# FFN2 products beside the last pair's seven-product gate and val: whole array in place of quarters

## The chip, the cores and the metric

The kernel runs on one core of one Trainium2 chip. The metric is the device time of that core in microseconds; the profile is one execution of the program, recorded on the chip. The engines are TensorE (PE for matmuls, PEld for its weight loads), VectorE (DVE), ScalarE (ACT), GpSimd (POOL) and SyncE (SP).

## The reference

Attention with a sigmoid in place of the softmax, then a SwiGLU block; batch 8, 12 heads, 448 tokens, head size 64, d_model 768, d_ff 1536, all in fp32 at the borders.

```python
scores = scale * np.matmul(q, k.transpose(0, 1, 3, 2)) - np.log(S)
attn = 1.0 / (1.0 + np.exp(-scores))
attn_out = np.matmul(attn, v)
x = attn_out.transpose(0, 2, 1, 3).reshape(B * S, H * D)      # 3584 x 768
g = x @ w_gate                                                # 3584 x 1536
silu = g * (1.0 / (1.0 + np.exp(-g)))
out = (silu * (x @ w_val)) @ w_out                            # 3584 x 768
```

## The kernel before

The work is cut by batch element (448 tokens) and, for the second matrix product, by pair of batch elements (896 tokens, four pairs m = 0 to 3).

**Attention.** For each batch element and each group of four heads, `burst` computes scores in quarters of the array (64 x 64 blocks, four matmuls at a time), `sig` applies the sigmoid on ScalarE, and `pv` multiplies with v. The results become the transposed x tiles `xT`.

**Gate and val (FFN1).** For batch elements 0 to 5, `f1` computes gate and val for two column blocks f and f + 1 together in quarters. For the last pair (elements 6 and 7), `f1_pair` uses a scheme of seven block products in place of eight: sums and differences of x tiles (`xsum`, on VectorE) and of weight blocks (`f1_sums`, made earlier, parked in DRAM and loaded back into the staging buffers by `wload`) are multiplied, and the products are added up again. `one_set(f)` issues, for each f of six, seven products of gate and seven of val. Each product is three matmuls of 128 x 128 weights by 448 columns on the whole array (line 727). Between them, products are copied out of PSUM by ScalarE (`snap`, line 741), added by VectorE (`add`, line 756), passed through the SiLU by ScalarE (`silu`, line 766) and multiplied by VectorE (`fin`, lines 775 and 778), which gives `hT`.

**FFN2.** For pair m, `f2_set(m, k)` handles two token tiles of 128 (`e`, the even, and `o`, the odd), again with seven products for eight. Each product contracts six blocks of 128 with 384 output columns. Products 5 and 6 use sums of hT tiles, s1 and s2, made by VectorE (lines 886 and 889); product 7 needs s3 (line 892), product 3 needs s4 (line 959). The results are taken out of PSUM by ScalarE (product 1, line 952) and VectorE (the others, line 912, the operations u2, u3, u4, c11, c12, c21, c22), and stored by DMA (line 922) from GpSimd's queue, or from SyncE's and ScalarE's for the last pair.

A product can be issued in two ways. `f2_single` issues six matmuls of 128 x 128 weights by 384 columns (line 903). `f2_pair` issues two products together in quarters, by `quarters` (line 549): 48 matmuls of 64 x 64 weights by 384 columns in two halves of 24. In each half two rows of quarters work on different products, and the second half exchanges the rows. The first matmuls of the second half wait for a `turn` (line 531), an empty instruction on ScalarE that waits for the last matmuls of the first half. Both products are evacuated after the second half.

**Order of work.** All work is first recorded as `op` objects with an engine, an estimated duration, dependencies and buffers. `list_schedule` then plays the list through with these estimates and writes out each engine's instructions in the order that comes of it. PSUM banks (tag "P", eight of them) are given to whoever is first able to start. The planner adds SWITCH = 0.094 us when TensorE changes between the whole array (mode "F") and quarters (mode "Q"), and while in quarters it prefers to remain there. FFN2 items stand in the list `f2q`; in the last stretch up to MIX = 3 items are recorded behind each f of the last pair's gate and val, and KEEP = 3 are held back for the end. This happens in the block that starts when `i == NQ and sl == 3`. The items issued there are those of pair m = 2; pair m = 3 comes last, and was issued by `f2_single` already.

Of the kernel before, what the change touches and what calls it, by code (L numbers as in the profile page):

```python
# [66 lines left out]
MARGIN = 1.0  # L67
# [131 lines left out]
def kernel(  # L199
# [17 lines left out]
    NS = 7  # L217
    QB = H // 4
# [8 lines left out]
    one = ctx.enter_context(tc.tile_pool(name="one", bufs=1))  # L227
# [44 lines left out]
    def op(*a, **kw):  # L272
        o = Op(*a, **kw)
        ops.append(o)
        return o
# [23 lines left out]
    R = {}  # L299
# [98 lines left out]
    def tr_pe(i, n, parts=None, split=False):  # L398

        ins = R[("cq", "ck")[n], i]  # L400
        parts = parts or [("DVE", 0, NS)]

        def fpe(s0, s1):
            def fn():
                if s0 == 0 or split:
                    T["tr", i, n] = bank("ps_tr").bitcast(BF16)[:, 0:NS * 128].rearrange("p (s c) -> p s c", s=NS)
                T["tr", i, n, s0] = T["tr", i, n]
                for s in range(s0, s1):
                    nc.tensor.transpose(out=T["tr", i, n][:, s, :],
                                        in_=src16[i % NSRC][:, n, s].rearrange("p a d -> p (a d)"),  # L410
                                        identity=idn)
            return fn

        def fm(eng, s0, s1):
            def fn():
                if n == 0 and s0 == 0:
                    qkT_tile(i)
                cp(eng, T["qkT", i][:, n, s0:s1], T["tr", i, n, s0][:, s0:s1])
            return fn
        for k, (eng, s0, s1) in enumerate(parts):  # L420
            a = op("PE", 0.06 * (s1 - s0), fpe(s0, s1),
                   deps=[(ins[min(k, len(ins) - 1)], -MARGIN if i > QB else 0.0)],
                   take=["P"] if s0 == 0 or split else [], give=R["cq", i][0].take if n and s1 == NS else [])
            if s0 == 0 or split:
                taken = a.take
            m = op(eng, 0.1 + (0.53 if eng == "DVE" else 0.8) * (s1 - s0) / NS, fm(eng, s0, s1), deps=[a],
                   take=["qkT"] if n == 0 and s0 == 0 else [], give=taken if s1 == NS or split else [])
            R.setdefault(("qkT", i), []).append(m)
            R["qkT", i, n, s0] = m
# [193 lines left out]
    NC = KC // 2  # L623
# [35 lines left out]
    def f1_pair(m):  # L659

        b0, b1 = 2 * m, 2 * m + 1
# [15 lines left out]
        def xsum(k, j):  # L677
            e0, e1, o0, o1 = (lambda: T["xT", b0, j]), (lambda: T["xT", b0, NC + j]), \
                (lambda: T["xT", b1, j]), (lambda: T["xT", b1, NC + j])
            out, x, y, f = {1: (lambda: tile_of(1, j), o0, o1, ADD),  # L680
                            2: (lambda: tile_of(2, j), lambda: tile_of(1, j), e0, SUB),
                            3: (o0, e0, o0, SUB),
                            4: (lambda: tile_of(4, j), e1, lambda: tile_of(2, j), SUB)}[k]
            deps = [R["xT", b, q] for b in (b0, b1) for q in (j, NC + j)] + quiet
            X[k, j] = op("DVE", 0.36, lambda: nc.vector.tensor_tensor(out=out(), in0=x(), in1=y(), op=f),
                         deps=deps + [X.get((k - 1, j))], take=["xT"] if (k, j) == (4, 2) else [])

# [168 lines left out]
    def f2_set(m, k):  # L856
# [51 lines left out]
        def add(name, n, dst, other, deps, free=True, first=None):  # L908
            def fn():
                if first:  # L910
                    first()
                nc.vector.scalar_tensor_tensor(out=c(*dst), in0=T["p", m, k, n], scalar=HREC, in1=c(*other), op0=MULT, op1=ADD)  # L912
            C[name] = op("DVE", 0.45, fn,
                deps=[P[n]] + deps, give=taken[n] if free else [])
# [26 lines left out]
        def after(n, final):  # L941

            def result(t):
                T[("osb",) + t] = staging("osf")[:, 0:DM] if final else \
                    sb.tile([128, DM], FP32, tag="osb", bufs=slots["osb"], name=f"osb_{t[0]}_{t[1]}")

            if n == 1:
                def fn(cols):
                    def go():
                        if cols == lo:  # L950
                            result(e)
                        nc.scalar.activation(out=c(e, cols), in_=T["p", m, k, 1], func=COPY, scale=HREC)
                    return go
                C["p1"] = op("ACT", 0.45, fn(lo), deps=[P[1]], take=["osf" if final else "osb"])
                C["p1b"] = op("ACT", 0.45, fn(hi), deps=[C["p1"]], give=taken[1])
            elif n == 6:
                add("u2", 6, (e, hi), (e, hi), [C["p1b"]])
            elif n == 2:
                C["s4"] = op("DVE", 0.56, lambda: nc.vector.tensor_tensor(
                    out=blk(e, 1), in0=blk(e, 1), in1=T["s", 2, m, k], op=SUB), deps=[P[2], C["s2"]])  # L960
                add("c11", 2, (e, lo), (e, lo), [C["p1"]])
                if end:
                    store(e, [C["c11"]], [], final, lo)
            elif n == 7:
                add("u3", 7, (o, lo), (e, hi), [C["u2"]], first=lambda: result(o))
                C["u3"].take = [Slot("osf" if final else "osb")]
            elif n == 5:
                add("u4", 5, (e, hi), (e, hi), [C["u3"]], free=False)
                add("c22", 5, (o, hi), (o, lo), [C["u3"]])
                P[5].give = P[5].give + C["s1"].take  # L970
                if end:
                    store(o, [C["c22"]], [], final, hi)
            elif n == 3:
                add("c12", 3, (e, hi), (e, hi), [C["u4"]])
                store(e, [C["c11"], C["c12"]], C["p1"].take, final, hi if end else slice(0, DM))
            elif n == 4:
                add("c21", 4, (o, lo), (o, lo), [C["u3"], C["c22"]])
                store(o, [C["c21"], C["c22"]], C["u3"].take, final, lo if end else slice(0, DM))
            R.setdefault(("f2", m), []).append(P[n])
        return dict(start=start, product=product, after=after, spec=spec, P=P, taken=taken, key=(m, k))  # L980

    def f2_pair(x, y):

        two = (x, y)
        key = x[0]["key"] + x[1:]

        def make(final):
            for f, n in two:
                if n == 1:
                    f["start"](final)  # L990

            def fn(t):
                def go():
                    if t == 0:
                        for q, (f, n) in enumerate(two):
                            T[("p",) + f["key"] + (n,)] = bank("ps_o", q)[:, 0:HW]
                    quarters([[(T[("p",) + f["key"] + (n,)], f["spec"][n][0]()[:, x // 2, x % 2], f["spec"][n][1](x))
                              for f, n in two] for x in range(NH)], HALVES, t, key)
                return go
            a = None  # L1000
            for t in range(2):
                a = op("PE", 0.1625 * NH, fn(t), mode=("Q", "Q"), take=[] if t else ["P", "P"],
                       deps=[d for f, n in two for d in f["spec"][n][2]()] + ([turn(a, key + (0,))] if t else [(x, LAT["PE"] + LATE) for x in [R.get("turn")] if x]))
                banks = banks if t else a.take
            R["turn"] = a
            for q, (f, n) in enumerate(two):
                f["P"][n] = a
                f["taken"][n] = banks[q:q + 1]
            for f, n in two:
                f["after"](n, final)  # L1010
        return make

    def f2_single(f, n):

        def make(final):
            if n == 1:
                f["start"](final)
            f["product"](n, final)
            f["after"](n, final)
        return make  # L1020
# [78 lines left out]
    for i in range(NQ + QB + 2):  # L1099
        att = i < NQ  # L1100
        for sl in range(4):
# [50 lines left out]
            while len(f2q) > (KEEP if fpos == NPLAIN * NF else 0) and f2acc >= f2q[0][0] and ("ws", 4, NH - 2) in R:  # L1152
                w, fn = f2q.pop(0)
                f2acc -= w
                fn(False)
            if i == NQ and sl == 3:
                sums, wload, one_set = f1_pair(B // 2 - 1)
                sums()
                todo = [(nm, f) for f in range(NH) for nm in "gv"]
                for x in todo[:5]:  # L1160
                    wload(*x)
                last = None
                for f in range(NH):
                    last = one_set(f, last)
                    for _ in range(min(MIX, len(f2q) - KEEP)):
                        f2q.pop(0)[1](False)
                    for x in todo[5 + 2 * f:7 + 2 * f]:
                        wload(*x)
# [46 lines left out]
```

## Time and profile before

| what | value |
|---|---|
| median of 3 runs | 403.71 us (402.93 to 409.8) |
| profiled execution, its own time | 403.9 us |
| span of the profiled execution | 402.1 us |
| granted TensorE clock, mean | 1.000 |
| TensorE busy | 394.9 us (98%) |
| VectorE / ScalarE / GpSimd busy | 254.2 / 243.6 / 136.2 us |
| DMA | 76.91 MB, mean 191 GB/s |
| last pair's gate and val begin | 299.8 us after the span's start |
| FFN2 of the last pair, first line 903 product | 369.35 us |

The busy time of an engine is the time in which at least one of its instructions ran. Matmuls overlap: one of 64 x 384 shows 0.33 us though the next step starts 0.16 us later, so rates are read from start to start. A view called the chain of work follows what ended last back from the last instruction, to whatever released each step. L549, L727 and so on are lines of the kernel.

### The profile page before, as it was taken

How to read it: one execution, taken by the hardware profiler on the slowest of the kernel's cores; microseconds unless marked ns; L12 is line 12 of the kernel's file. 1: busy time of each engine (PE TensorE's matmuls, PEld its weight loads, DVE VectorE, ACT ScalarE, POOL GpSimd, SP SyncE). 2: the span in 40 equal slices, each digit the busy share in tenths (PEclk: the TensorE clock that was granted, in tenths of full speed). 3: DMA queues.
4: the chain of work that ended last, by engine and by line, in shares of the span. 5: the costliest groups of instructions: out<-in, count | busy, mean ns of one | idle time of the engine just before them, and what ended most of it. 6: DMA issues, size and time to landing. Idle time of an engine off the chain costs nothing.

```text
span 402.1 us, 15922 instructions
## 1 busy us (share of the span) xinstructions
PE 394.9 (98%) x6973; PEld 270.7 (67%) x6973; DVE 254.2 (63%) x492; ACT 243.6 (61%) x509; POOL 136.2 (34%) x202
## 2 busy tenths in 40 slices
PE   8999999999999999999999999999999999999995
PEld 3546657667797787799777866666885555555663
DVE  3525544546786465755866857576668666658874
ACT  5996687757766852766668666767726434663110
POOL 1788865565455223424234332402020202000100
PEclk9999999999999999999999999999999999999999
DMA  8999999999776629759678688853004325100535
GB/s 277 379 375 377 374 301 268 315 304 284 221 203 186 160 52 276 170 178 261 163 211 224 202 223 223 191 215 102 22 14 123 104 82 156 42 0 2 159 88 147
DMA packets 67989, 76.91 MB, mean 191 GB/s; under 512 B 35920, under 2 KB 61264, under 8 KB 67920
## 3 DMA queue, kind: packets, MB, share of 16 engines
q1 hardware_dynamic: 63952, 62.93, 54.4%
q0 software_dynamic: 1920, 7.87, 7.7%
q10 hardware_dynamic: 2048, 5.11, 3.3%
q8 instruction: 54, 0.88, 0.9%
q14 instruction: 15, 0.12, 0.1%
HBM read 51.90 MB, written 15.73 MB: 168 GB/s over the span
## 4 chain that ended last, share of the span: by engine, by line
PE 85%; DMA 11%; POOL 1%; SPq 1%; issue 0%; DVE 0%; POOLq 0%; ACTq 0%
PE ps_v L549 19%; PE ps_g L549 18%; PE ps_o L549 17%; PE ps_o L903 7%; PE ps_sc L452 6%; PE ps_pv L495 6%; DMA st<-in_v_dram 6%; PE ps_g L727 6%; PE ps_v L727 6%; DMA st<-in_moe_w_gate_dram 5%; SPq L325 1%; POOL v L295 1%; POOL wg L366 1%; DVE st L912 0%; POOLq L295 0%
## 5 line engine op out<-in xcount | busy, mean ns | idle before, releaser
L473 ACT ACTIVATE pt<-ps_sc 128x448 f16<-128x448 f32 x336 | 163.0, 552 | 57.6 <-PE ps_sc L452 57.1
L549 PE MATMUL ps_v<-xT,wv 64*64 64x448 f16 x1728 | 103.0, 349 | 0.4 <-issue 0.3
L549 PE MATMUL ps_g<-xT,wg 64*64 64x448 f16 x1728 | 101.7, 349 | 0.3 <-POOL wg L366 0.2
L549 PEld LDWEIGHTS <-wg 64*64 64x64 f16 x1728 | 66.2, 107 | 21.6 <-issue 1.1
L452 PE MATMUL ps_sc<-qkT 64*64 64x448 bf16 x672 | 80.4, 351 | 0.1
L549 PEld LDWEIGHTS <-wv 64*64 64x64 f16 x1728 | 65.7, 107 | 21.1 <-issue 1.9
L579 DVE TENSOR_TENSOR t<-ps_g,s 128x448 f16<-128x448 f32 x72 | 43.1, 620 | 52.1 <-ACT s L573 51.4
L549 PE MATMUL ps_o<-wo,hT 64*64 64x384 f16 x888 | 72.4, 324 | 0.1
L295 POOL CAST src<-st 128x896 bf16<-128x896 f32 (+1 forms) x43 | 41.4, 966 | 70.5 <-DMA st<-in_q_dram 33.1
L549 PEld LDWEIGHTS <-hT 64*64 64x64 f16 x1080 | 50.5, 107 | 11.7 <-issue 3.5
L295 POOL CAST v<-st 64x448 f16<-64x448 f32 (+1 forms) x72 | 41.0, 569 | 48.2 <-PE ps_pv L495 35.0
L586 DVE SCALAR_TENSOR_TENSOR hT<-ps_v,t 128x448 f16<-128x448 f32 x72 | 41.7, 618 | 23.4 <-PE ps_v L549 22.0
L922 POOL DMA_DIRECT2D out_dram<-osb x40 | 20.8, 525 | 96.4 <-DVE osb L912 96.2
L573 ACT ACTIVATE s<-ps_g 128x448 f16<-128x448 f32 x72 | 37.0, 549 | 23.1 <-PE ps_g L549 13.0
L495 PE MATMUL ps_pv<-pt,v 64*64 64x448 f16 x672 | 46.9, 350 | 0.1
L549 PE MATMUL ps_o<-st,s 64*64 64x384 f16 x480 | 46.3, 323 | 0.0
L912 DVE SCALAR_TENSOR_TENSOR osb<-ps_o,osb 128x384 f32<-128x384 f32 x70 | 36.6, 551 | 10.8 <-PE ps_o L549 9.0
L452 PEld LDWEIGHTS <-qkT 64*64 64x64 bf16 x672 | 35.1, 106 | 11.1 <-issue 2.4
L495 PEld LDWEIGHTS <-v 64*64 64x64 f16 x672 | 26.8, 107 | 9.9 <-issue 2.3
L549 PEld LDWEIGHTS <-s 64*64 64x64 f16 x480 | 29.1, 107 | 5.1 <-issue 1.5
L293 DVE CAST xT<-ps_pv 128x448 f16<-128x448 f32 x40 | 23.4, 618 | 12.6 <-PE ps_pv L495 11.0
L727 PEld LDWEIGHTS <-st 128*128 128x128 f16 x144 | 13.8, 98 | 13.6 <-issue 1.2
(78 smaller groups left out, 391.0 us busy)
## 6 DMA issues: line engine op xcount, KB each, us to landing
st<-in_q_dram SPq DMA_DIRECT2D x24, 448.0 KB, 5.5
st<-in_v_dram SPq DMA_DIRECT2D x24, 448.0 KB, 6.8
st<-in_k_dram SPq DMA_DIRECT2D x23, 448.0 KB, 6.1
out_dram<-osb POOLq DMA_DIRECT2D x40, 192.0 KB, 3.5
st<-in_moe_w_gate_dram SPq DMA_DIRECT2D x12, 384.0 KB, 9.0
st<-in_moe_w_val_dram SPq DMA_DIRECT2D x12, 384.0 KB, 8.8
st<-in_moe_w_out_dram SPq DMA_DIRECT2D x12, 384.0 KB, 7.8
tsum<-st ACTq DMA_DIRECT2D x12, 384.0 KB, 4.1
```

The source lines that it names most:

```text
L293: nc.vector.tensor_copy(out=o, in_=i)
L295: nc.gpsimd.tensor_copy(out=o, in_=i)
L452: nc.tensor.matmul(out=sc[a][64 * (g ^ a):64 * (g ^ a) + 64, 0:S].rearrange("k (s p) -> k s p", s=NS), lhsT=kT[r, s, 64 * g:64 * g + 64], ...
L473: nc.scalar.activation(out=T[("pt",) + key][:, a], in_=T[("sc",) + key][a][:, 0:S], func=SIGM, bias=sbias, scale=qkscale)
L495: nc.tensor.matmul(out=T["pv", i, a][64 * g:64 * g + 64, :], lhsT=T["v16", i][r, a, s, :], rhs=T["pt", i, s][r, a, :], start=(s == 0), sto ...
L549: mm = nc.tensor.matmul(out=o[cs], lhsT=w[rs, cs], rhs=x[rs], start=p == 0 and k == 0, stop=p == len(parts) - 1 and k == len(steps) - 1)
L573: nc.scalar.activation(out=t, in_=T["g", b, f], func=SIGM)
L579: nc.vector.tensor_tensor(out=t, in0=T["g", b, f], in1=T["s16", b, f], op=MULT)
L586: nc.vector.scalar_tensor_tensor(out=T["hT", m][:, f, o * S:(o + 1) * S], in0=T["v", b, f], scalar=HSC, in1=T["t1", b, f], op0=MULT, op1=MULT)
L727: nc.tensor.matmul(out=T["fp", key], lhsT=win(nm, f, n)()[:, j], rhs=xin[n](j), start=n in first and j == 0, stop=j == NC - 1, skip_group_ ...
L903: nc.tensor.matmul(out=T["p", m, k, n], lhsT=lhs()[:, x // 2, x % 2], rhs=rhs(x), start=x == 0, stop=x == NH - 1)
L912: nc.vector.scalar_tensor_tensor(out=c(*dst), in0=T["p", m, k, n], scalar=HREC, in1=c(*other), op0=MULT, op1=ADD)
```

## The change

When the last pair's gate and val begin, a flag is set. From then on, an item that would have been a pair in quarters records its two products one after the other through `f2_single`. Three added conditions on the planner's order (a lead of 99 us leaves only "not before it has started") concern transposes, their copies and the operation c22; one on `xsum` would add the last element's `f1` as a dependency, where it has one.

```diff
@@ tr_pe
-                   deps=[(ins[min(k, len(ins) - 1)], -MARGIN if i > QB else 0.0)],
+                   deps=[(ins[min(k, len(ins) - 1)], -MARGIN if i > QB else 0.0)] + [(x, 99.0) for x in R.get(("tr", i, n), [])],
...
+            R.setdefault(("tr", i, n), []).append(a)
...
-            m = op(eng, 0.1 + (0.53 if eng == "DVE" else 0.8) * (s1 - s0) / NS, fm(eng, s0, s1), deps=[a],
+            m = op(eng, 0.1 + (0.53 if eng == "DVE" else 0.8) * (s1 - s0) / NS, fm(eng, s0, s1), deps=[a] + [(x, 99.0) for x in R.get(("qkT", i), [])[:1]],
@@ f1_pair, xsum
-            deps = [R["xT", b, q] for b in (b0, b1) for q in (j, NC + j)] + quiet
+            deps = [R["xT", b, q] for b in (b0, b1) for q in (j, NC + j)] + quiet + R.get(("F1", b1), [])
@@ f2_set, after
-                add("c22", 5, (o, hi), (o, lo), [C["u3"]])
+                add("c22", 5, (o, hi), (o, lo), [C["u3"], (C["u4"], 99.0)])
@@ f2_pair
         def make(final):
+            if R.get("full"):
+                for one in two:
+                    f2_single(*one)(final)
+                return
             for f, n in two:
@@ main loop
             if i == NQ and sl == 3:
+                R["full"] = True
                 sums, wload, one_set = f1_pair(B // 2 - 1)
```

## The prediction

> **What bounds the kernel now.** First I read the busy lines, the clock and the chain that ended last on the page. They say whether any engine but TensorE can matter.
>
> ```profile
> PE 394.9 (98%) x6973; PEld 270.7 (67%) x6973; DVE 254.2 (63%) x492; ACT 243.6 (61%) x509; POOL 136.2 (34%) x202
> ...
> PEclk9999999999999999999999999999999999999999
> ...
> PE 85%; DMA 11%; POOL 1%; SPq 1%; issue 0%; DVE 0%; POOLq 0%; ACTq 0%
> ```
>
> TensorE is busy in 98% of the span at the full clock. The DMA part of the chain lies at the start (transfers up to 49.4 us). So a microsecond of TensorE time saved later is a microsecond of the end, unless it becomes a wait. Next I read the chain in order of time where the changed products run, from 306.8 us on (start, length, what):
>
> ```profile
> 305.70 0.57 PE ps_g L727 x3
> 306.26 0.57 PE ps_v L727 x3
> 306.83 1.10 PE ps_o L549 x24
> 307.93 0.67 PE ps_g L727 x3
> 308.61 0.57 PE ps_v L727 x3
> 309.17 0.57 PE ps_g L727 x3
> 309.74 0.57 PE ps_v L727 x3
> 310.31 2.07 PE ps_o L549 x48
> 312.38 0.68 PE ps_g L727 x3
> 313.06 2.07 PE ps_o L549 x48
> 315.13 0.68 PE ps_v L727 x3
> ...
> 365.99 2.10 PE ps_o L549 x48
> 368.09 0.02 issue
> 368.11 0.02 ACTq L531
> 368.14 0.04 issue
> 368.18 1.17 PE ps_o L549 x24
> 369.35 28.39 PE ps_o L903 x174
> ```
>
> The chain stays on TensorE from 299.8 to 397.75 us. A group "L549 x24" is one half of a pair (24 quarter products), "L727 x3" one product of the last pair's gate or val, "L903 x6" one FFN2 product on the whole array. Three prices stand here. A whole-array FFN2 product costs 28.39 / 29 = 0.979 us. A gate or val product after another costs 0.567 us. The first one after quarters costs 0.67 to 0.68. A lone half costs 1.10.
>
> **The change, part by part.** The instruction order of the built changed kernel shows where it acts. Up to the half at 306.83 us every engine's instructions and waits are the same; GpSimd's and SyncE's are the same to the end. So the new scheduling conditions on transposes, sums and c22 move nothing: zero, by that order. From 306.83 us on, nine pairs (18 halves, 432 quarter matmuls) become 18 whole-array products (108 matmuls). The 74 gate and val products left there stay. Where halves stood in groups of 1, 2, 2, 1, the products now stand in groups of 1 and 5.
>
> *Bare products: nothing gained.* A half does the arithmetic of one product. In the timeline of the last halves its four quarters advance by 0.16 us per step (368.37, 368.53, 368.69), six steps, 0.96 us; the whole-array product takes 0.976 from start to start (370.27 to 371.24). The array was as full before as it is after.
>
> *Going in and out of quarters: the gain.* Before, TensorE left the whole array for quarters 12 times from 306.83 on: seven lone halves, four groups of two, and a last group of three.
> - Lone half: 1.10 - 0.979 = 0.12 going in, and 0.675 - 0.567 = 0.11 on the product after it: 0.23, seven times, 1.61 us.
> - Group of two: 2.07 - 1.958 = 0.11, and 0.11 behind it: 0.22, four times, 0.89 us.
> - Last group: 368.18 + 1.17 - 365.99 = 3.36 us for three halves, less 2.94 = 0.42 us. It holds the one wait on ScalarE's turn mark (368.09 to 368.18), as the last half had nothing between it and the one whose end it needs.
>
> Sum: 1.61 + 0.89 + 0.42 = 2.9 us. The other way: the stretch 306.83 to 369.35 is 62.5 us; filled with 74 x 0.567 = 42.0 and 18 x 0.979 = 17.6 it is 59.6. Again 2.9 us.
>
> *What replaces it.* A gate or val product directly beside an FFN2 product on the whole array (24 such borders) does not occur before. Nearest rows: gate to val, which changes bank, weights and operand, adds nothing (0.57 after 0.57), and FFN2 to FFN2 neither (29 products in one stretch). The far end is the border to quarters, 0.11 to 0.12 a side, 2.7 us in all; below zero is excluded, since the products already follow without a gap. I take zero, as the rows without a mode change are nearer, and keep 2.7 for the range.
>
> *Weight loads.* A quarter load took 106 ns and ran beside other quarters; a whole-array load takes 98 ns and must hide behind a 163 ns matmul. In 370 to 397 us there are 168 matmuls in 27.0 us, 0.161 each, with 167 such loads: they hide. The Trainium skill speaks against the change here: "TensorE: Matmul & The Clock Gate", section "Part 3: Packing small matmuls — row/col tiling", says a weight load overlaps running matmuls only when its row group differs, which whole-array products never offer. By that rule alone, 108 loads of 98 ns would stand bare, some 10.6 us, and the kernel would end near 411.6 us. The row of 370 to 397 us contradicts it for this form, so I use the row.
>
> *What hides the evacuation.* VectorE was busy 42.1 of 62.5 us there; in 59.6 us that is 71%. The tight places are the runs of five FFN2 products. In the first, by start distances of before (0.535 us for an accumulate of 448 columns, 0.31 for the f16 multiply, 0.47 for FFN2's), VectorE has three accumulates, one multiply and eight FFN2 operations, 5.7 us, beside 4.9 us of TensorE. It finishes about 1.1 us behind the run's last product. The next gate accumulate needs its own two products and a ScalarE copy, about 0.8 us later still, and each bank that TensorE takes was released more than 0.5 us earlier by the same walk. So: zero. The second run is looser, since its first product (6) has no sums waiting. In the last run (7, 5, 3, 4, then the final pair's 1 and 6) product 6 needs the sum s2. From the end of val's product 7 as zero: s1 6.34 to 6.81, c12 to 7.28, s2 to 7.75; the product would start at 8.12. Before, s2 ended at 369.10, 1.17 us ahead of 370.27. So the cover shrinks to about 0.3 us; if the walk errs, 0.1 to 0.3 us is lost. Then the s3 and s4 that follow are no later relative to TensorE than before.
>
> *ScalarE's queue.* The turn marks of the nine pairs go; one of them is worth 0.09 us, inside the 0.42. Loads and stores keep their order on SyncE and GpSimd and only start up to 2.9 us earlier; DMA share in this stretch is 0.23.
>
> After 369.35 us the order is that of before, so the end moves as a whole: span 402.1 - 2.9 = 399.2. The profiled execution took 403.9, 1.8 more than its span, and the median of the runs is 403.71. By the one the forecast is 401.0, by the other 400.8; I take **400.9 us**, 0.7% faster. About 2% is what a measurement of this kernel can tell from no change (its three runs spread from 402.93 to 409.8), so this is expected to count as the same.
>
> **The rivals.**
> 1. *The borders cost what the quarters' borders cost.* For: no row shows an L727 product touching an L903 one. Against: every border inside the whole-array mode that is shown adds nothing. It gives back 24 x 0.11 = 2.7 us: 403.6 us.
> 2. *VectorE becomes the bound (the slower side).* Place: the three runs of five. If TensorE cannot take a bank until VectorE has caught up, each run costs the 1.1 us that VectorE is behind: 3.3 us, net +0.4, 404.2 us; at twice that lag, 407.6 us. It decides against the change once the three waits sum to over 2.9 us. For: FFN2 products now come five in a row where at most two did, and one VectorE operation evacuates each at 0.47 us besides the sums. Against: eight banks, of which five or six are free as the run begins, and 21.6 busy of 27 us in the last stretch, where 28 products follow each other without a stall.
> 3. *Whole-array weight loads are not hidden.* 108 x 98 ns = 10.6 us, less 2.9: 411.6 us. Against it stands the row of 370 to 397 us.
> 4. *The change does nothing.* Excluded: the built order holds 324 fewer matmuls.
>
> **How the numbers follow.** Forecast, with small losses in the last run: 0.80. Borders: 0.10. VectorE: 0.06. Weight loads: 0.02. Some other gain (a hole closing elsewhere) or loss: 0.02. The range: from 399.9, the forecast less the 1.0 us between the fastest run (402.93) and the profiled one (403.9), to 403.6, the far end of the border cost. Faster by over 2% (under 395.6 us) would need 5 us more than there is: 0.01. Slower by over 2% (over 411.8): 0.02. Within: 0.97.
>
> **What would show it.** Right: no L549 after about 306.8 us; groups of L903 x6 and x30 between L727 groups at 0.98 us a product; every L727 product at 0.57, also behind L903; the final 174 matmuls starting near 366.4 us. Rival 1 would show as 0.67 behind each FFN2 group; rival 2 as waits of TensorE on VectorE in front of ps_o or ps_g groups; rival 3 as L903 products of 1.5 us. I would be wrong if TensorE waited for s2 by over 1 us, or if the granted clock left 1.00 in the longer whole-array stretch; the two such stretches shown (342 to 361 and 370 to 397 us) kept 1.00.

## The result

The changed kernel takes 401.48 us (median of 22 runs, 399.48 to 403.69) against 403.74 us for the kernel before (22 runs, 402.17 to 409.8). The ratio of the two, taken over the fast runs (without the two slowest of before, 408.55 and 409.8 us), is 0.9934, with a 95% interval of 0.9912 to 0.9956: 0.66% faster, some 2.7 us (1.8 to 3.6). That is clear of zero and, by the 2% mark, counts as the same. The profiled execution took 400.04 us, with a span of 398.3 us.

The span is 3.8 us shorter, but not all of that is the change. The first gate product of the last pair, up to which the instructions of the two kernels are the same, starts at 299.84 us before and at 298.84 us here. In the profiles of the runs below it starts between 298.56 and 300.96 us where that part is unchanged. So about a microsecond of the 3.8 belongs to the one execution. I therefore compare a length inside the span: from that first gate product to the start of the last 174 FFN2 matmuls. It was 369.35 - 299.84 = 69.51 us. After, the last 192 matmuls start at 362.67 and run at 31.21 / 192 = 0.1626 us each, so the last 174 start at 365.60 and the length is **66.76 us**: 2.75 us less. A little more lies behind that point: before, the 174 matmuls follow a stay in quarters and take 28.39 us; after, they follow whole-array products and take 28.28 (up to 393.88). From the first gate product to the end of TensorE's work it is 397.75 - 299.84 = 97.91 us before and 393.88 - 298.84 = 95.04 us after: 2.87 us less.

The page of the changed kernel: busy time, share and instructions of each engine, and the granted clock of TensorE.

```profile
PE 391.2 (98%) x6647; PEld 268.2 (67%) x6649; DVE 254.0 (64%) x492; ACT 243.4 (61%) x509; POOL 136.7 (34%) x202
...
PEclk9999999999999999999999999999999999999999
```

TensorE's matmuls are 326 fewer by the records (324 by the built order) and its busy time follows the span; the other engines have the same work. The chain in order of time (start, length, what), through the first stretch that changed and at its end:

```profile
302.42 0.58 PE ps_g L728 x3
...
304.22 1.28 ACT L767
305.50 0.01 issue
305.51 0.58 ACT pt L767
306.10 0.02 issue
306.12 0.39 DVE hT L779
306.51 0.47 DVE s L890
306.98 0.54 DVE pt L757
307.51 0.47 DVE hT L893
307.98 0.55 DVE hT L757
308.52 0.04 issue
308.57 0.73 PE ps_v L728 x3
309.30 4.88 PE ps_o L904 x30
314.17 0.57 PE ps_g L728 x3
...
319.85 0.97 PE ps_o L904 x6
320.82 0.57 PE ps_g L728 x3
...
362.67 31.21 PE ps_o L904 x192
```

(The lines of this kernel named here stand one below those of before: L728 is the gate and val product, L904 the FFN2 product, L757 the accumulate of gate and val.) Five FFN2 products now cost 4.88 us, 0.976 each, and the gate product behind them 0.57, not 0.67 as behind quarters. The detour of the chain through ScalarE and VectorE is new: TensorE waits there. The timeline of TensorE shows how long.

```profile
307.77 0.54 PE L728 MATMUL ps_g<-src,wg 128*128 128x448 f16 x2
308.15 0.35 PE L728 MATMUL ps_g<-xT_s,wg 128*128 128x448 f16 x1
308.57 0.54 PE L728 MATMUL ps_v<-src,wv 128*128 128x448 f16 x2
308.94 0.35 PE L728 MATMUL ps_v<-xT_s,wv 128*128 128x448 f16 x1
309.13 1.14 PE L904 MATMUL ps_o<-wo,hT 128*128 128x384 f16 x6
```

The step after 308.15 is 0.42 us where one matmul takes 0.19: 0.23 us lost in front of val's product 3 of the first f.

### The profile page after: what moved, and what is told of

Read it like the earlier page. It is cut to its first block, busy times and chain, and to the rows that moved or that the text cites. A ratio compares the mean times of both kernels' runs of the same rounds, so it can differ in the third digit from the quotient of the medians.

```text
span 398.3 us, 15268 instructions
## 1 busy us (share of the span) xinstructions
PE 391.2 (98%) x6647; PEld 268.2 (67%) x6649; DVE 254.0 (64%) x492; ACT 243.4 (61%) x509; POOL 136.7 (34%) x202
## 4 chain that ended last, share of the span: by engine, by line
PE 84%; DMA 10%; POOL 2%; DVE 2%; ACT 1%; issue 0%; POOLq 0%; SPq 0%; ACTq 0%
PE ps_v L550 19%; PE ps_g L550 18%; PE ps_o L550 12%; PE ps_o L904 12%; PE ps_pv L496 6%; PE ps_sc L453 6%; PE ps_v L728 5%; PE ps_g L728 5%; DMA st<-in_v_dram 5%; DMA st<-in_moe_w_gate_dram 4%; DMA st<-in_q_dram 1%; POOL wg L366 1%; POOL v L295 1%; ACT pt L474 0%; ACT L767 0%
## 5 line engine op out<-in xcount | busy, mean ns | idle before, releaser
L550 PE MATMUL ps_v<-xT,wv 64*64 64x448 f16 x1728 | 101.8, 350 | 0.0
L550 PEld LDWEIGHTS <-wg 64*64 64x64 f16 x1728 | 65.0, 107 | 22.4 <-POOL wg L366 1.2
L550 PEld LDWEIGHTS <-wv 64*64 64x64 f16 x1728 | 63.9, 107 | 21.7 <-issue 1.0
L453 PE MATMUL ps_sc<-qkT 64*64 64x448 bf16 x672 | 78.1, 351 | 0.1
L550 PE MATMUL ps_o<-wo,hT 64*64 64x384 f16 x648 | 51.9, 323 | 0.1
L550 PEld LDWEIGHTS <-hT 64*64 64x64 f16 x792 | 39.5, 107 | 5.9 <-issue 0.7
L453 PEld LDWEIGHTS <-qkT 64*64 64x64 bf16 x672 | 33.5, 107 | 10.8 <-issue 1.9
L550 PE MATMUL ps_o<-st,s 64*64 64x384 f16 x336 | 32.7, 323 | 0.0
L904 PEld LDWEIGHTS <-hT 128*128 128x128 f16 x186 | 18.1, 98 | 12.5 <-issue 0.4
L904 PE MATMUL ps_o<-wo,hT 128*128 128x384 f16 x138 | 25.7, 326 | 0.0
```

Of the source, the lines that this page charges most:

```text
L453: nc.tensor.matmul(out=sc[a][64 * (g ^ a):64 * (g ^ a) + 64, 0:S].rearrange("k (s p) -> k s p", s=NS), lhsT=kT[r, s, 64 * g:64 * g + 64], ...
L550: mm = nc.tensor.matmul(out=o[cs], lhsT=w[rs, cs], rhs=x[rs], start=p == 0 and k == 0, stop=p == len(parts) - 1 and k == len(steps) - 1)
L904: nc.tensor.matmul(out=T["p", m, k, n], lhsT=lhs()[:, x // 2, x % 2], rhs=rhs(x), start=x == 0, stop=x == NH - 1)
```

## The experiments

All edits are shown against the changed kernel, and each ratio is to the kernel before, run beside it on the same chip, with its 95% interval. Most compare the same length, from the first gate product of the last pair to the start of the last 174 FFN2 matmuls: 69.51 us before, 66.76 after. Where another measure is used, the text says so.

**Pairs kept, but on the whole array (e1).** Each half of a pair is one whole product; the joint banks, the turn mark and the joint evacuation stay.

```diff
-            if R.get("full"):
-                for one in two:
-                    f2_single(*one)(final)
-                return
+            full = R.get("full")
...
+                    if full:
+                        f, n = two[t]
+                        for x in range(NH):
+                            mm = nc.tensor.matmul(out=T[("p",) + f["key"] + (n,)], lhsT=..., rhs=..., ...)
+                            if t and x == 0:
+                                after_ins(mm.ins, T["turn", key + (0,)])
+                        T["end", key + (t,)] = [mm.ins]
+                        return
...
-                a = op("PE", 0.1625 * NH, fn(t), mode=("Q", "Q"), ...
+                a = op("PE", 0.1625 * NH, fn(t), mode=("F", "F") if full else ("Q", "Q"), ...
```

> The nine pairs keep their form (two products recorded together, two banks taken at once, the second product waiting for the turn mark on ScalarE, both evacuated after the second), but each half is one product on the whole array; all work is done. The length compared is from the first gate product of the last pair to the start of the last 174 FFN2 matmuls: 69.5 us before, 66.8 us in the changed kernel. Theory (the gain is the going in and out of quarters): 66.6 to 67.1 us, ratio to before 0.993. Rival (the gain is the end of the joint evacuation and of the turn marks): 69 us or more, ratio 0.999 to 1.002.

Measured: ratio 0.9928 (0.9903 to 0.9952); 367.99 - 300.96 = 67.03 us. The groups stand as before (1, 2, 2, 1), and the chain shows what each of them costs now:

```profile
325.20 1.95 PE ps_o L1002 x12
327.15 0.57 PE ps_g L728 x3
...
364.79 1.96 PE ps_o L1002 x12
366.75 0.02 issue
366.77 0.02 ACTq L532
366.79 0.05 issue
366.84 1.15 PE ps_o L1002 x6
367.99 28.29 PE ps_o L904 x174
```

A group of two takes 1.95 in place of 2.07, and the product of gate or val behind it 0.57 in place of 0.67 to 0.68. So the gain comes with the array's mode, in the old structure too. The only part that the structure keeps is the turn mark of the last group: 0.09 us of waiting and a last half of 1.15 in place of 0.976, together 0.27 us, which is what the length exceeds 66.76 by. (It is one delay: the last half starts at 366.84, 1.24 us behind the product ahead of it, which starts at 365.60. The chain books a part of it to the half, since the recorded ends of matmuls overlap the next starts.)

**Three of nine pairs back in quarters (e5).**

```diff
             if i == NQ and sl == 3:
-                R["full"] = True
...
                     last = one_set(f, last)
+                    R["full"] = f > 0
```

> The flag is set only after the first three pairs beside gate and val, so six of nine pairs are whole-array; all work is done. Theory: four of the twelve stays in quarters come back, two lone halves and two groups of two, 2 x 0.23 + 2 x 0.22 = 0.90 us, less the 0.2 us that TensorE waits in the changed kernel in front of val's product 3 of the first f: 67.3 to 67.6 us from the first gate product to the last 174 matmuls (66.8 in the changed kernel, 69.5 before). Rival (the gain sits in one place, the last group with its turn mark): 66.8 or less.

Measured: ratio 0.9939 (0.9917 to 0.9960). The first gate product starts at 300.52, the last 192 matmuls at 365.05, the last 174, 18 matmuls or 2.93 us later, at 367.98: 67.46 us, inside the 67.3 to 67.6 expected. The gain grows with the number of stays in quarters that are taken away; it doesn't sit in one place.

**Whole array everywhere (e3).** Here the time of whole runs is compared, since products move from one stretch to another.

```diff
+    R["full"] = True
     for i in range(NQ + QB + 2):
```

> The flag is set from the start, so all pairs of FFN2 are issued as single products on the whole array, also those between FFN1's quarters; all work is done. In the built order TensorE changes between quarters and the whole array 74 times in place of 34. Theory: 40 changes at 0.11 us cost 4.4 us against the changed kernel: about 405.4 us, ratio to before 1.004 (1.001 to 1.008), and each such group costs its whole-array time plus about 0.22. Rival (a product on the whole array is cheaper in itself): 25 more pairs gain 0.3 us each, 394 us, ratio 0.975.

Measured: 403.75 us, ratio 1.0007 (0.9991 to 1.0023). The rival is far off: 25 more pairs on the whole array bring no gain but lose most of what nine had gained, some 2.9 us. The chain, where FFN1's and attention's quarters surround the products:

```profile
222.48 0.19 PE ps_sc L453 x4
222.67 2.06 PE ps_o L904 x12
224.72 0.31 PE ps_sc L453 x4
```

Two products take 2.06 (1.95 without a change of mode) and the score matmuls behind them 0.31 in place of 0.19: 0.11 + 0.12 us, the same price from the other side. The size was missed, though: 20 more stays at 0.22 are 4.4 us, and 2.9 (1.8 to 4.0 by the two intervals together) were measured; the ratio lies just under the 1.001 to 1.008 expected. The profiles do not close the gap of 1.5 us. Two val halves of FFN1 that take 1.43 us in place of 1.14 before and after (at 120.71 and 132.74 us after) have no counterpart here, up to 0.6 us; but in the second profile of the changed kernel the first of them takes 1.25, so they differ from one execution to the next. And TensorE stands 0.53 us in front of gate's product 7 of the first f, where it waits on a copy by ScalarE; that is new and makes the gap larger. What fills it is not settled.

**The table of the SiLU loaded early (e4).**

```diff
                 sums()
+                op("ACT", 1.5, lambda: nc.scalar.activation(out=warm, in_=sb_t, func=SILU), deps=R["sigmoids"])
```

> The changed kernel plus one SiLU of a single column on ScalarE, placed after the last sigmoid, so that the table that the first SiLU needs is loaded earlier; all work is done. Theory (the 0.23 us that TensorE stands in front of val's product 3 of the first f comes from that 1.28 us load, through VectorE's queue): the load ends before the first copy of gate's product 1, the wait goes, 66.5 us from the first gate product to the last 174 matmuls against 66.8. Rival (VectorE is late there of itself, by the FFN2 operation that now stands in its queue): the wait stays, 66.7 to 66.8.

Measured: ratio 0.9918 (0.9899 to 0.9938); 363.83 + 2.93 - 300.22 = 66.54 us. The chain has no detour left, and the load stands in a free stretch of ScalarE:

```profile
293.78 1.28 ACT L1165 ACT_TABLE_LOAD   x1
295.08 0.20 ACT L1165 ACTIVATE warm<-sbiast 128x1 f32<-128x1 f32 x1
...
305.48 0.57 ACT L767 ACTIVATE pt<-pt 128x448 f16<-128x448 f32 x1
```

The wait of 0.23 us was the load's: with it gone the length is 2.97 us below that of before, and the stretch to the end of TensorE's work (395.05 - 300.22 = 94.83 us) 3.08 us below. The FFN2 operation in VectorE's queue, the rival, stands behind the accumulate in question and had no part.

**Column halves: another mode than quarters (e6).**

```diff
+                    if cols:
+                        for z in (slice(0, 64), slice(64, 128)):
+                            nc.tensor.matmul(out=T["p", m, k, n][z], lhsT=lhs()[:, x // 2, x % 2][:, z], rhs=rhs(x), ...)
+                        continue
...
+            cols = R.get("cols")
...
             if R.get("full"):
+                R["cols"] = True
                 for one in two:
                     f2_single(*one)(final)
+                R["cols"] = False
                 return
```

> The changed kernel, but each of the 18 products is issued as column halves: two matmuls of 128 x 64 weights by 384 columns, all rows, beside each other; all work is done. The order has eight stays away from the whole array (groups of 1, 5, 1, 5, 1, 1, 1 and 3 products), with no turn marks and no joint evacuation. Theory (leaving and re-entering the whole-array mode costs, whatever the other mode is): 8 x 0.22 = 1.8 us over the changed kernel, 68.3 to 68.8 us from the first gate product to the last 174 matmuls (66.8 in the changed kernel, 69.5 before). Rival (the cost belongs to the quarters with their exchange of rows): 66.8 us. If the two halves don't run beside each other, 18 x 0.98 = 18 us are added instead.

Measured: ratio 0.9973 (0.9954 to 0.9991); 367.00 - 298.76 = 68.24 us, just under the range.

```profile
305.18 0.57 PE ps_v L728 x3
305.74 1.10 PE ps_o L906 x12
306.84 0.67 PE ps_g L728 x3
...
309.21 5.00 PE ps_o L906 x60
314.21 0.67 PE ps_g L728 x3
```

A lone product costs 1.10 and the gate product behind it 0.67, to the digit as with quarters; five cost 5.00 in place of 4.88. The two halves run beside each other. Eight stays at 0.22 are 1.8 us; 1.48 were added. The 0.23 us wait on the table load is gone, as TensorE now comes that much later to val's product 3, and the way back behind the last stay lies in the last 174 matmuls, which take 28.40 us here (395.40 - 367.00) as before. So the price is paid for leaving the whole-array form, whether for quarters or for halves.

The weight loads show where that price sits. Before, the first load for the gate product behind the lone half starts at 307.86 us, together with its matmul (307.86) and after 0.30 us without a load; in the changed kernel the load for the same product starts at 306.48, 0.16 us ahead of its matmul (306.64). It is so at every change of form from the first gate product on, to quarters and back before, to column halves and back here: load and matmul start within 0.01 us of each other, and the step to that matmul is 0.09 us longer than without a change. A load takes 0.10 to 0.11 us. That the price is mainly this one load, no longer hidden, is a reading of these rows; no run here separates it from other causes.

**One more pair, and the early table (e7).** The changed kernel again (e8) ran beside it.

```diff
+            if i == NQ and sl == 2:
+                R["full"] = True
             while len(f2q) > (KEEP if fpos == NPLAIN * NF else 0) and ...
...
                 sums()
+                op("ACT", 1.5, lambda: nc.scalar.activation(out=warm, in_=sb_t, func=SILU), deps=R["sigmoids"])
```

> The changed kernel, the table of the SiLU loaded early as in e4, and the flag set one step earlier, so that the pair of which one half lay alone between the first gate and val products is whole-array too; all work is done. Theory: one more stay goes (0.22 us) and the wait on the table load (0.23 us): 0.45 us less than the changed kernel, ratio to before about 0.992, and no product of gate and val longer than 0.57 us in the profile except the first. Rival (what is saved there comes back as a wait, since seven gate and val products now start in a row): the same as the changed kernel.

> The changed kernel itself, beside e6 and e7 on the same chip: ratio to before 0.991 to 0.996; 66.7 to 66.9 us from the first gate product to the last 174 matmuls, with TensorE's wait of 0.23 us in front of val's product 3 of the first f again (theory), or 66.5 us without it (if that wait was an accident of one execution).

Measured: 0.9949 (0.9932 to 0.9966) for the one with both, 0.9937 (0.9917 to 0.9957) for the changed kernel again. Here the length needs another start, as a product moved ahead of the first gate product: from the last group of attention's 28 matmuls of line 496 it is 364.02 + 2.93 - 294.11 = 72.84 us, and 362.39 + 2.93 - 292.04 = 73.28 us for the changed kernel. The forecast 0.45 us are there in the profile (0.44), and TensorE runs without a wait through the stretch. In the time of whole runs they don't show: the ratio forecast, 0.992, lies outside the interval, and the intervals of e7 and e8 overlap widely, so 0.1% can't be told from them either way. The changed kernel's own length is 365.32 - 298.56 = 66.76 us again, with the same 0.23 us wait (a step of 0.42 at 307.87), so that wait is no accident.

## Why the prediction was right, and what it missed

**Bound and sum.** The forecast was 2.9 us off the end, by the going in and out of quarters; measured are 2.87 us from the first gate product to the end of TensorE's work, and 2.7 (1.8 to 3.6) in the time. The forecast of 400.9 us stands 0.6 below the median. The mechanism is shown by e1, e5 and e6. That 2.87 comes so close to 2.9 is partly luck: with the early table the gain is 3.08, so the sum was some 0.2 us short, and the wait described below took 0.2 back. The sum left out the way back to the whole array behind the last group, 0.1 us; that sat instead in the price of a whole-array product, 28.39 / 29 = 0.979, where 0.976 is the rate from start to start, and made 18 products some 0.06 us too dear.

**Bare products.** Right: 0.976 us on the whole array, and pairs gain or lose nothing by themselves. Where the surrounding work is in quarters, the whole array loses (the run with all pairs).

**The border between gate and val products and FFN2 products.** The value taken, zero, holds at every one: 0.57 before and behind "L904 x6" and "x30". (The one 0.73, at 308.57, follows the wait; from start to start it is 0.56, 308.57 to 309.13.) Rival 1 falls.

**Weight loads.** In the 31.10 us from 362.7 to 393.8 us there are 192 matmuls, 0.162 each, with whole-array loads between them: hidden. The granted clock stayed at 1.00 there and from 306 to 366 us. The rule of the Trainium skill ("TensorE: Matmul & The Clock Gate", section "Part 3: Packing small matmuls — row/col tiling") that a load overlaps running matmuls only with another row group is contradicted for whole-array loads here too, and the 10.6 us worked out from it didn't come. The same section also lets a load into the background weight buffer run ahead of the matmuls, which fits this row.

**Evacuation.** The walk through the runs of five held. VectorE's queue in and behind the first run, and in the last one:

```profile
314.44 0.55 DVE L893 TENSOR_TENSOR hT<-hT 128x768 f16<-128x768 f16 x1
315.98 0.62 DVE L757 SCALAR_TENSOR_TENSOR pt<-ps_g,pt 128x448 f32<-128x448 f32 x1 [1.00 <-PE ps_g L728]
...
366.53 0.55 DVE L890 TENSOR_TENSOR s<-s,hT 128x768 f16<-128x768 f16 x1
```

VectorE is done 0.98 us behind the first run's end (314.99 against 314.01; 1.1 was forecast), and then waits a whole microsecond for TensorE, so rival 2 has nothing to price. In the last run s2 ends at 367.08 and product 6 starts at 367.38: 0.3 us of cover, as worked out, and no wait.

**The step that failed: "What hides the evacuation".** It put the tight places into the runs of five and at s2, and took zero. It didn't walk the products of gate and val that stand between a lone FFN2 product and the first run. In the first f, val's product 3 adds onto the bank that VectorE reads in the accumulate of product 5. In the kernel before, the accumulate and val's product 3 stood so in the timelines of VectorE and TensorE:

```profile
308.90 0.62 DVE L756 SCALAR_TENSOR_TENSOR hT<-ps_v,pt 128x448 f16<-128x448 f32 x1
...
309.58 0.54 PE L727 MATMUL ps_v<-src,wv 128*128 128x448 f16 x2
```

The accumulate ended at 309.52: 0.06 us of cover. After, it is this line:

```profile
307.90 0.62 DVE L757 SCALAR_TENSOR_TENSOR hT<-ps_v,pt 128x448 f16<-128x448 f32 x1
```

It starts 9.06 us behind the first gate product in both kernels (308.90 - 299.84, 307.90 - 298.84), so VectorE is no later than it was. Here the lone FFN2 product ahead of it and the gate product behind that cost 0.23 us less, TensorE came 0.23 us earlier, and it waited 0.23 us. The chain behind the accumulate begins at the 1.28 us table load of the first SiLU, which had been hidden as long as the stay in quarters was there to be paid. So the first lone half's 0.23 of the sum was not gained. The early table shows it by taking the cause away.

**Turn marks.** I put 0.42 us on the last group, with 0.09 us of waiting in it. The pairs on the whole array show 0.27 us for the mark, from start to start, and the kernel before shows the same: at the mark its quarters step by 0.44 us (367.74 to 368.18) in place of 0.16. The sum is untouched, its division was off.

## What to carry to other kernels

When two kinds of matmul alternate, count how often TensorE changes between the whole array and a split of it, and price each stay by the excess of the group itself and of the first group behind it. Here that is 0.22 us per stay from either side, and arithmetic per product is the same; so products take the form of their neighbours: whole beside whole, quarters beside quarters. When time is taken out ahead of an accumulation, look for the next wait behind it in the first pass, where one-off costs such as a table load sit.

## What was not expected of the hardware

A split into two column halves, with all rows in use, cost as much at its borders as quarters do (1.10 us for a product of 0.976, 0.67 for the gate product behind it of 0.57), and ran as fast in between (5.00 for five, of which 0.12 is the way in). And 1.28 us of table load on ScalarE, an engine that is 61% busy, reached TensorE only through five VectorE operations that stood in order behind it.
